# Another order for the seven products of a gate or up matrix, with each PSUM bank's two products eight apart

## Chip, cores and metric

The kernel runs on one core of one Trainium2 chip. The metric is device time in microseconds (us) of one launch, the median of several runs. On the core work five engines with queues of their own: TensorE (PE in the profile, its weight loads PEld), VectorE (DVE), ScalarE (ACT), GpSimd (POOL) and SyncE (SP), which issues most of the transfers.

## What is computed

The reference is a block of two branches on a normalised input of 2048 rows and 576 columns. All inputs are float32.

```python
def _B_ref(x, w_gate, w_up, w_down):
    g = jnp.einsum("bsd,df->bsf", x, w_gate)
    u = jnp.einsum("bsd,df->bsf", x, w_up)
    h = _gelu(g) * u
    return jnp.einsum("bsf,fd->bsd", h, w_down)

xn = _layernorm(x, axis=-1)
s = _A_ref(xn, A_wqkv, A_wo)
g = _silu(_B_ref(xn, B_w_gate, B_w_up, B_w_down))
return x + s * g
```

`_A_ref` is linear attention with 32 heads of 18 columns. `w_gate` and `w_up` are 576 x 4608, `w_down` is 4608 x 576. The change touches only the part with `w_gate` and `w_up`.

## The kernel before

The program has three stages on PE: the attention branch, the gate and up matrices, and the down product. The middle stage is cut into 18 groups of 256 hidden columns. Each group has a gate matrix and an up matrix, so there are 36 matrices in all, numbered `q` from 0 to 35; even `q` is a gate matrix, odd `q` an up matrix.

**One matrix.** A matrix product of 2 x 2 blocks is done with seven block products in place of eight (Strassen's scheme in Winograd's form). `STEPS` (L814) lists the seven as steps `k` = 0 to 6: the name of an accumulator, a weight operand and an input operand. `S1` to `S4` and `T1` to `T4` are sums of blocks. Each step is done for two halves of the rows, `s` = 1 and then `s` = 0, so a matrix is 14 products. In the profile, operands called `xo_` belong to `s` = 1 and those called `xr_` to `s` = 0; weights `wa` hold A11, S1, S2, S3 and weights `wb` hold A12, A22, S4.

**Accumulators.** There are four pairs of PSUM banks: `al`, `be`, `ga`, `de`, one bank of a pair for each `s`. Steps 0 and 4 both add into `al`, steps 2 and 5 into `ga`, steps 3 and 6 into `de`, step 1 alone uses `be`. After the first product of a bank its sum is read and kept, and the second product is then added on top in the bank. `bank_of` (L825) gives each name its banks; `al` and `be` exchange theirs from matrix to matrix.

**PE's order.** `roll` (L832) cuts PE into four groups of 32 rows that work side by side. Each product is 27 matmuls of 32 rows by 512 columns, 6 or 7 for each group of rows. Group 1 begins a product only when group 0 has finished it, and so on, so four or more products are on their way at a time. In one slot every group does one matmul; a product is begun every 6 or 7 slots, and a matrix takes 94 or 95. PE's queue is in order: a matmul that waits holds all four groups.

**Reading a product.** `matrix` (L886) says what follows each product. Let `b` be the bank and `u`, `c22` two SBUF tiles per `s`. Step 0: ACT copies `al` to `u`. Step 1: DVE adds `be` to `u`. Step 2: DVE writes `c22 = u + ga`. Step 3: DVE adds `de` to `c22`, which finishes one block. Step 4 finishes a block from `al`. Steps 5 and 6: DVE adds `u` and `ga`, or `u` and `de`, each of which finishes a block. For a gate matrix "finish" (L919) is an ACT Gelu in place in a tile `h`; for an up matrix (L945) it is a DVE multiply into `h`. In the profile `c22` has the name `h` in a gate matrix and `u` in an up matrix. At step 5 and 6 of an up matrix POOL makes sums of `h` (rows `hs<-h,h`, `h<-h`, `hs<-h,hs`), and SP stores `h` and these sums to `hs_d` in DRAM (rows `hs<-h`, `hs<-hs`) for the down stage.

**Preparing the next matrix.** After certain steps (`run(todo[k])`) the operands of the next matrix are cut into two float32r words: ACT writes the first word, DVE two subtractions of the second (`cut_w`, L786). A11 is cut behind step 0 (`wa<-raw`), S1 to S3 together behind step 3 (`wa<-sm`), A12 and A22 behind step 4 (`wb<-raw`), S4 behind step 5 (`wb<-sm`). POOL forms the sums S (`sm`, L774) and, once per group, sums of `w_down` (`td`, L979).

All operations are pinned to program order on each engine. Tiles and banks are guarded by semaphores: the first matmul into a bank waits until the last reader of that bank is done.

Of the kernel before, what the change touches and what calls it, by code (L numbers as in the profile page):

```python
# [25 lines left out]
TT = TBN // P  # L26
# [39 lines left out]
def block_kernel(ctx, tc, x, xe, xt_d, wq_d, wkv0_d, wkv1_d, wkv2_d, wo, wgu_d, wd_d, out):  # L66
# [8 lines left out]
    def bank_at(i, name):  # L75
        return ps.tile([P, 512], F32, tag=f"bk{i}", bufs=1, name=name)
# [29 lines left out]
    def vec(op, *args, **kw):  # L106
        pin(getattr(nc.vector, op)(*args, **kw))  # L107
# [685 lines left out]
    def mat_pieces(q):  # L793
# [18 lines left out]
        ]  # L812

    STEPS = (  # L814
        ("al", "A11", "B11"), ("be", "S2", "T2"), ("ga", "S1", "T1"), ("de", "S3", "T3"),
        ("al", "A12", "B21"), ("ga", "S4", "B22"), ("de", "A22", "T4"),
    )
    NS = len(STEPS)

    def pairs_of(wn, xn, t, empty):  # L820

        jobs = [(0, 0), (0, 3), (3, 0), (1, 1), (1, 4), (4, 1)]
        return jobs if t == empty else jobs + [(2, 2)]

    def bank_of(q, bk, s):  # L825

        i = SBS.index(s)
        if bk in ("al", "be"):
            return i + (6 if (bk == "al") == (q % 2 == 0) else 0)
        return i + (2 if bk == "ga" else 4)  # L830

    def roll(matrix_of):  # L832

        todo, lens = [], [0] * 4
        for q in range(NQ):
            for k, (bk, wn, xn) in enumerate(STEPS):
                for s in SBS:
                    free = [t for t in range(4) if t not in (W_LO[wn], X_LO[xn])]
                    empty = max(free, key=lambda t: lens[t])
                    jobs = [pairs_of(wn, xn, t, empty) for t in range(4)]  # L840
                    lens = [lens[t] + len(jobs[t]) for t in range(4)]
                    todo.append((q, k, s, jobs))
        rows = [[(p, n) for p, w in enumerate(todo) for n in range(len(w[3][t]))] for t in range(4)]
        begins = [[0] for t in range(4)]
        for q, k, s, jobs in todo:
            for t in range(4):
                begins[t].append(begins[t][-1] + len(jobs[t]))
        skew = [0]
        for t in range(3):
            skew.append(2 + skew[t] + max(  # L850
                begins[t][p + 1] - begins[t + 1][p] for p in range(len(todo))))
        bs, mats = {}, {}
        sems = [tc.alloc_semaphore(f"tile_{t}") for t in range(3)]
        for n in range(skew[3] + len(rows[3])):
            for t in range(4):
                i = n - skew[t]
                if not 0 <= i < len(rows[t]):
                    continue
                p, j = rows[t][i]
                q, k, s, jobs = todo[p]  # L860
                bk, wn, xn = STEPS[k]
                first = t == 0 and j == 0
                if first and k < 4:
                    bs[q, bk, s] = bank_at(bank_of(q, bk, s), f"{bk}_{q}_{s}")
                wi, xi = jobs[t][j]
                last = t == 3 and j == len(jobs[t]) - 1
                r = group(t)
                i = mm(
                    bs[q, bk, s], w_at(q, wn)[r, wi, :], X[s][xn][r, xi, :],
                    start=(first and k < 4), stop=last, skip_group_check=True,  # L870
                    tile_position=(t * KR, 0),
                )
                if t > 0 and j == 0:
                    i._wait_ge(sems[t - 1], p + 1)
                if t < 3 and j == len(jobs[t]) - 1:
                    i.then_inc(sems[t])
                    tc.no_tile_sem_insts.add(i.ins.name)
                    tc.add_to_no_dep_group(f"row_{p}", i.ins)
                if last:
                    tc.declare_fence(i.ins, group=f"row_{p}")  # L880
                if last:
                    if k == 0 and s == SBS[0]:
                        mats[q] = matrix_of(q)
                    mats[q](k, s, bs[q, bk, s])

    def matrix(q, c22, done, todo):  # L886

        u = {}

        def step(k, s, b):  # L890
            if k == 0:
                u[s] = tmp([P, TBN], f"u_{q}_{s}")
                act(u[s], b, AF.Copy)
            elif k == 1:
                vec("tensor_add", u[s], u[s], b)
            elif k == 2:
                vec("tensor_add", c22(s), u[s], b)
            elif k == 3:
                vec("tensor_add", c22(s), c22(s), b)
                done(s, 1, 1, None)  # L900
            elif k == 4:
                done(s, 0, 0, b)
            elif k == 5:
                done(s, 0, 1, (u[s], b))
            else:
                done(s, 1, 0, (u[s], b))
            if s == SBS[-1]:
                run(todo[k])

        return step  # L910
# [206 lines left out]
    def down_all():  # L1117
# [5 lines left out]
        for n in range(N2):  # L1123
            k, g = divmod(n, NG)
            if g == 0 and k in (0, 2, 3, 5):
                accs = [(own_bank if i < 2 else bank)(f"bd_{k}_{i}") for i in range(2 * TT)]
            if g == 0 and k in (1, 4, 5, 6):
                sx[k] = load_sx(k, (14, 15) if k in (1, 5) else (2, 6))
            if k == 6 and g == NG - AHEAD:
                break  # L1130
            load_t(chunk_of(min(n + 8, N2 - 1)) + 1)
            prep_t(chunk_of(min(n + 3, N2 - 1)) + 1)
            prep_s(n + 3)
            down_mm(n, range(2 * TT), accs)
            load_s(n + 6)
            run(late, 2)
            if g < NG - 1:
                continue
            run(late)
            for j in range(2 * TT):  # L1140
                p = accs[j][:, 0:HALF]
                if k == 0:
                    act(u[:, j], p, AF.Copy)
                elif k == 1:
                    yt[k] = yt.get(k) or big(3, [P, 2 * TT, HALF], F32, f"y_{k}")
                    act(yt[k][:, j], p, AF.Silu)
# [299 lines left out]
        return (gate_matrix if q % 2 == 0 else up_matrix)(g, todo)  # L1446

    roll(matrix_of)
    turns["one"] = 0
    load_s(5)  # L1450
    down_all()

# [54 lines left out]
```

## Time and profile before

| what | value |
|---|---|
| median of 3 runs | 1552.02 us (1548.44 to 1553.24) |
| the profiled execution, its own time | 1549.51 us |
| span of the profile in it | 1547.8 us |
| granted TensorE clock | 0.998 |
| gate and up stage, first matmul to the down stage's first | 284.4 to 1139.7 us |
| down stage | 403.6 us |

The profile's rows give start, duration, engine, line, operation, `out<-in` by the program's names without buffer numbers, and in square brackets how long the engine had been idle and what released it. A DVE, ACT or POOL row with "x2" is two instructions in a row. An idle time under 0.15 us is not shown. Since the helpers record each operation, nearly all rows have the helper's line (L104 ACT, L107 DVE, L110 PE, L115 POOL), and one tells them apart by the tiles.

### The profile page before, as it was taken

Reading aid. Unit: us, or ns where it says so; the run is one execution under the profiler, and the core shown is the slowest. Engines: PE = TensorE matmul, PEld = TensorE weight load, DVE = VectorE, ACT = ScalarE, POOL = GpSimd, SP = SyncE. Lnnn points to the kernel's source line nnn. Section 1 sums busy time; section 2 is a strip of 40 time slices with the busy share of each in tenths; the row PEclk is TensorE's granted clock in tenths of the full one; section 3 lists DMA queues with packets and bytes.
Section 4 is the critical chain, followed back from the end, with each engine's and each line's share of the span. In section 5 each row is a group of like instructions: output and inputs, shape, how many; then the busy total and the mean of one; then the engine's idle time right before and its main releaser. Section 6 shows DMA issues by size and latency. Waiting matters only on the chain. (4 is left out here: it accounts for less than half of the span.)

```text
span 1547.8 us, 42471 instructions
## 1 busy us (share of the span) xinstructions
PE 1506.8 (97%) x18431; PEld 1360.0 (88%) x18431; DVE 1044.2 (67%) x1579; ACT 566.5 (37%) x1047; POOL 544.4 (35%) x520
## 2 busy tenths in 40 slices
PE   9999999999999999999999999999999999999998
PEld 8989989888787788778888888877789999999998
DVE  7676566376677776677766776866784565555765
ACT  5444455323222132232233222222234555444443
POOL 5452521243465543555434645435410020000220
PEclk9999999999999999999999999999999999999999
DMA  5354014632344323443423443333578757777773
GB/s 229 127 220 159 1 59 184 252 134 106 128 168 158 143 105 114 156 168 133 151 96 127 169 168 133 114 114 146 202 263 273 241 161 265 244 263 248 276 244 129
DMA packets 114549, 261.97 MB, mean 169 GB/s; under 512 B 10218, under 2 KB 38634, under 8 KB 112314
## 3 DMA queue, kind: packets, MB, share of 16 engines
q1 hardware_dynamic: 112586, 249.95, 45.5%
q0 software_dynamic: 1632, 8.91, 1.6%
q8 instruction: 144, 2.36, 0.6%
q14 instruction: 43, 0.35, 0.1%
q10 hardware_dynamic: 144, 0.39, 0.1%
HBM read 161.27 MB, written 97.91 MB: 167 GB/s over the span
## 5 line engine op out<-in xcount | busy, mean ns | idle before, releaser
L1072 PEld LDWEIGHTS bd<-t,s 128*128 128x128 f32 x3024 | 403.5, 189 | 0.6 <-issue 0.6
L1072 PE MATMUL bd<-t,s 128*128 128x288 f32 x3024 | 403.7, 296 | 0.0
L110 PE MATMUL ga<-xo_B,wb 32*128 32x512 f32 x972 | 258.1, 397 | 17.2 <-DVE h L107 14.6
L110 PE MATMUL de<-xo_T,wa 32*128 32x512 f32 x972 | 259.1, 394 | 10.6 <-DVE u L107 10.6
L110 PE MATMUL al<-xo_B,wb 32*128 32x512 f32 x972 | 265.4, 397 | 0.0
L110 PE MATMUL al<-xr_B,wb 32*128 32x512 f32 x972 | 262.2, 397 | 0.0
L110 PE MATMUL ga<-xr_B,wb 32*128 32x512 f32 x972 | 257.0, 395 | 3.2 <-DVE h L107 3.1
L110 PE MATMUL de<-xr_T,wa 32*128 32x512 f32 x972 | 258.8, 395 | 0.0
L107 DVE TENSOR_TENSOR s<-sr,s 128x512 fp32r<-128x512 f32 x252 | 176.1, 739 | 122.6 <-ACT s L104 118.0
L110 PE MATMUL ga<-xr_T,wa 32*128 32x512 f32 x972 | 253.7, 390 | 0.0
L110 PE MATMUL de<-xr_T,wb 32*128 32x512 f32 x972 | 248.5, 390 | 2.2
L110 PE MATMUL de<-xo_T,wb 32*128 32x512 f32 x972 | 248.7, 390 | 0.0
L110 PE MATMUL ga<-xo_T,wa 32*128 32x512 f32 x972 | 248.3, 387 | 0.0
L110 PE MATMUL al<-xr_B,wa 32*128 32x512 f32 x972 | 248.3, 387 | 0.0
L110 PE MATMUL be<-xr_T,wa 32*128 32x512 f32 x972 | 245.8, 387 | 0.0
L110 PE MATMUL al<-xo_B,wa 32*128 32x512 f32 x972 | 244.4, 386 | 0.0
L110 PE MATMUL be<-xo_T,wa 32*128 32x512 f32 x972 | 243.7, 385 | 0.0
L104 ACT ACTIVATE s<-sr 128x512 fp32r<-128x512 f32 x252 | 149.1, 625 | 193.6 <-PE bd L1072 138.9
L110 PEld LDWEIGHTS ga<-xo_B,wb 32*128 32x128 f32 x972 | 171.4, 183 | 39.5 <-DVE h L107 22.2
L110 PEld LDWEIGHTS de<-xr_T,wb 32*128 32x128 f32 x972 | 175.3, 183 | 23.2 <-DVE h L107 9.9
L110 PEld LDWEIGHTS de<-xo_T,wa 32*128 32x128 f32 x972 | 174.0, 183 | 22.7 <-DVE u L107 17.8
L110 PEld LDWEIGHTS ga<-xr_B,wb 32*128 32x128 f32 x972 | 172.7, 183 | 23.5 <-DVE h L107 10.9
(174 smaller groups left out, 4245.9 us busy)
## 6 DMA issues: line engine op xcount, KB each, us to landing
sr<-hs SPq DMA_DIRECT2D x252, 256.0 KB
hs<-h SPq DMA_DIRECT2D x68, 512.0 KB
raw<-in_wgu_dram SPq DMA_DIRECT2D x36, 768.0 KB
hs<-hs SPq DMA_DIRECT2D x102, 256.0 KB
td<-in_wd_dram SPq DMA_DIRECT2D x18, 576.0 KB
td<-td SPq DMA_DIRECT2D x18, 576.0 KB
tr<-td SPq DMA_DIRECT2D x16, 576.0 KB
tr<-in_wd_dram SPq DMA_DIRECT2D x12, 576.0 KB
```

The source lines that it names most:

```text
L104: pin(nc.scalar.activation(*args, **kw))
L107: pin(getattr(nc.vector, op)(*args, **kw))
L110: i = nc.tensor.matmul(*args, **kw)
L1072: nc.tensor.matmul(banks[j][:, 0:HALF], hw[n, s][:, a, t * P : (t + 1) * P], w[:, c, g % 4], start=(new and g == 0 and m == 0), stop=(g == ...
```

## The change

`STEPS` gets another order: the product S2 x T2 with its accumulator `be` moves from step 1 to step 3, and the `ga` and `de` products of steps 2 and 3 move up to steps 1 and 2. Now `al` has steps 0 and 4, `ga` 1 and 5, `de` 2 and 6, `be` 3. Between the two products of a bank there were 8 (`al`) or 6 (`ga`, `de`) products of PE's order from start to start, and now there are 8 for each. `bank_of` gives the pairs of banks in turn, moved on by one pair from matrix to matrix; from the last use of a pair to its use in the next matrix there are then 8 products as well.

The readers follow: `c22` begins as an ACT copy of `ga`, DVE adds `de` to it at step 2, and at step 3 DVE adds `be` to `u` and then `u` to `c22`. The down stage names its banks 0 to 7 in order, as the last matrix frees them.

```diff
     STEPS = (
-        ("al", "A11", "B11"), ("be", "S2", "T2"), ("ga", "S1", "T1"), ("de", "S3", "T3"),
+        ("al", "A11", "B11"), ("ga", "S1", "T1"), ("de", "S3", "T3"), ("be", "S2", "T2"),
         ("al", "A12", "B21"), ("ga", "S4", "B22"), ("de", "A22", "T4"),
     )
...
-    def bank_of(q, bk, s):
-
-        i = SBS.index(s)
-        if bk in ("al", "be"):
-            return i + (6 if (bk == "al") == (q % 2 == 0) else 0)
-        return i + (2 if bk == "ga" else 4)
+    def bank_of(q, k, s):
+
+        return 2 * ((k - q) % 4) + SBS.index(s)
...
             elif k == 1:
+                act(c22(s), b, AF.Copy)
+            elif k == 2:
+                vec("tensor_add", c22(s), c22(s), b)
+            elif k == 3:
                 vec("tensor_add", u[s], u[s], b)
-            elif k == 2:
-                vec("tensor_add", c22(s), u[s], b)
-            elif k == 3:
-                vec("tensor_add", c22(s), c22(s), b)
+                vec("tensor_add", c22(s), c22(s), u[s])
                 done(s, 1, 1, None)
...
-                accs = [(own_bank if i < 2 else bank)(f"bd_{k}_{i}") for i in range(2 * TT)]
+                accs = [bank_at(i, f"bd_{k}_{i}") for i in range(2 * TT)]
```

What moves in the queues is shown at two places. The first is DVE in the up matrix 15, from the cut of A11 for the next matrix up to the cut of S1 to S3. Names carry group, half and buffer number: `u_15_1` is the tile `u` of matrix 15 for `s` = 1, `u22_7_1` is its `c22` (of group 7), and `be_15_1` is the bank. Before:

```order
L107 TENSOR_TENSOR u_15_1_9865<-u_15_1_9865,be_15_1_9743 128x512
L107 TENSOR_TENSOR u_15_0_9896<-u_15_0_9896,be_15_0_9777 128x512
L107 TENSOR_TENSOR u22_7_1_9980<-u_15_1_9865,ga_15_1_9808 128x512
L107 TENSOR_TENSOR u22_7_0_10006<-u_15_0_9896,ga_15_0_9839 128x512
L107 TENSOR_TENSOR u22_7_1_9980<-u22_7_1_9980,de_15_1_9875 128x512
L107 TENSOR_TENSOR h_7_1_1_9423<-h_7_1_1_9423,u22_7_1_9980 128x512
L107 TENSOR_TENSOR u22_7_0_10006<-u22_7_0_10006,de_15_0_9905 128x512
L107 TENSOR_TENSOR h_7_0_1_9425<-h_7_0_1_9425,u22_7_0_10006 128x512
L107 TENSOR_TENSOR wa_2921<-sm_16_9860,wa_2921 128x3x256
```

The same place on DVE after the change:

```order
L107 TENSOR_TENSOR u22_7_1_9958<-u22_7_1_9958,de_15_1_9840 128x512
L107 TENSOR_TENSOR u22_7_0_9984<-u22_7_0_9984,de_15_0_9871 128x512
L107 TENSOR_TENSOR u_15_1_9893<-u_15_1_9893,be_15_1_9903 128x512
L107 TENSOR_TENSOR u22_7_1_9958<-u22_7_1_9958,u_15_1_9893 128x512
L107 TENSOR_TENSOR h_7_1_1_9453<-h_7_1_1_9453,u22_7_1_9958 128x512
L107 TENSOR_TENSOR u_15_0_9924<-u_15_0_9924,be_15_0_9937 128x512
L107 TENSOR_TENSOR u22_7_0_9984<-u22_7_0_9984,u_15_0_9924 128x512
L107 TENSOR_TENSOR h_7_0_1_9455<-h_7_0_1_9455,u22_7_0_9984 128x512
L107 TENSOR_TENSOR wa_2921<-sm_16_9888,wa_2921 128x3x256
```

The number of DVE operations is the same. Behind the last of the first four products there were four operations up to the cut, and now there are six, in two chains of three that depend on each other; two of the adds have both inputs in SBUF.

The second place is ACT in the gate matrix 16, from the copy of `al` to the first word of S1 to S3 for the next matrix. Before:

```order
L104 ACTIVATE u_16_1_10322<-al_16_1_10108 128x512
L104 ACTIVATE u_16_0_10353<-al_16_0_10143 128x512
L104 ACTIVATE wa_2921<-raw_17_10129 128x384
L104 ACTIVATE h_8_1_1_10319<-h_8_1_1_10319 128x512
L104 ACTIVATE h_8_0_1_10321<-h_8_0_1_10321 128x512
L104 ACTIVATE wa_2921<-sm_17_10313 128x3x384
```

The same place on ACT after the change:

```order
L104 ACTIVATE u_16_1_10356<-al_16_1_10142 128x512
L104 ACTIVATE u_16_0_10387<-al_16_0_10177 128x512
L104 ACTIVATE wa_2921<-raw_17_10163 128x384
L104 ACTIVATE h_8_1_1_10353<-ga_16_1_10213 128x512
L104 ACTIVATE h_8_0_1_10355<-ga_16_0_10256 128x512
L104 ACTIVATE h_8_1_1_10353<-h_8_1_1_10353 128x512
L104 ACTIVATE h_8_0_1_10355<-h_8_0_1_10355 128x512
L104 ACTIVATE wa_2921<-sm_17_10347 128x3x384
```

Two copies from the banks `ga` have come in ahead of the Gelu of the same tiles; they write the tiles `h` one step earlier than DVE did.

More of the change, by code (lines that the diff above doesn't have):

```diff
@@ L814, in block_kernel @@
     STEPS = (
-        ("al", "A11", "B11"), ("be", "S2", "T2"), ("ga", "S1", "T1"), ("de", "S3", "T3"),
+        ("al", "A11", "B11"), ("ga", "S1", "T1"), ("de", "S3", "T3"), ("be", "S2", "T2"),
         ("al", "A12", "B21"), ("ga", "S4", "B22"), ("de", "A22", "T4"),
     )
-    NS = len(STEPS)
     def pairs_of(wn, xn, t, empty):
@@ L863, in roll @@
                 if first and k < 4:
-                    bs[q, bk, s] = bank_at(bank_of(q, bk, s), f"{bk}_{q}_{s}")
+                    bs[q, bk, s] = bank_at(bank_of(q, k, s), f"{bk}_{q}_{s}")
                 wi, xi = jobs[t][j]
@@ L1448, in block_kernel @@
     roll(matrix_of)
-    turns["one"] = 0
     load_s(5)
```

## The prediction

> **What bounds the kernel now.** I read the page first, then the groups of PE by line, the timeline of PE for one gate and one up matrix, and the timelines of DVE and POOL beside them. The first fence has the page's head and its engine line, then two rows of PE's groups (busy, mean ns, idle before and who ended it), then where the stage with the change begins (the first `al` matmul at 284.4) and ends (the chain of waits: the first `bd` matmul).
>
> ```profile
> span 1547.8 us, 42471 instructions
> PE 1506.8 (97%) x18431; PEld 1360.0 (88%) x18431; DVE 1044.2 (67%) x1579; ACT 566.5 (37%) x1047; POOL 544.4 (35%) x520
> L110 PE MATMUL ga<-xo_B,wb 32*128 32x512 f32 x972 | 258.1, 397 | 17.2 <-DVE h L107 14.6 <-DVE u L107 0.2
> L110 PE MATMUL de<-xo_T,wa 32*128 32x512 f32 x972 | 259.1, 394 | 10.6 <-DVE u L107 10.6
> L110 PE MATMUL al<-xo_B,wa x972: 382/385/497, 284.4 to 1118.1; 32*128 32x512 f32 x195
> 1139.74 403.63 PE bd L1072 x3024
> ```
>
> PE is busy 97% of the span, but its matmuls overlap, so this share hides lost time. The stage takes 1139.74 - 284.4 = 855.3 us for 36 matrices. PE's own idle time there is put down to DVE: 17.2 us before the second `ga` product, 10.6 before the first `de` product. The timeline of PE shows the true loss, from the first matmul of gate matrix 16 on.
>
> ```profile
> 660.07 0.39 PE L110 MATMUL al<-xo_B,wa 32*128 32x512 f32 x1
> 670.19 0.49 PE L110 MATMUL de<-xo_T,wa 32*128 32x512 f32 x1 [0.62 <-DVE u L107]
> 677.51 0.49 PE L110 MATMUL ga<-xo_B,wb 32*128 32x512 f32 x1 [0.89 <-DVE h L107]
> 677.85 0.39 PE L110 MATMUL ga<-xo_B,wb 32*128 32x512 f32 x1
> 684.90 0.39 PE L110 MATMUL al<-xo_B,wa 32*128 32x512 f32 x1
> 691.02 0.39 PE L110 MATMUL ga<-xo_T,wa 32*128 32x512 f32 x1
> 694.19 0.39 PE L110 MATMUL de<-xo_T,wa 32*128 32x512 f32 x1
> 700.62 0.49 PE L110 MATMUL ga<-xo_B,wb 32*128 32x512 f32 x1
> 707.25 0.39 PE L110 MATMUL al<-xo_B,wa 32*128 32x512 f32 x1
> ```
>
> In the up matrix from 684.90 to the first `de` matmul at 694.19 nothing waits: 41 slots in 9.29 us, 0.2266 us a slot. A gate matrix has 95 slots, an up matrix 94, so without waits they would take 21.53 and 21.30 us. They take 24.83 and 22.35: 3.30 and 1.05 us are lost, **4.35 us a pair, 78 us for 18 pairs**. In the gate matrix the first 41 slots take 10.12, so the wait at 670.19 costs 0.83, and 0.11 more for restarting (677.51 to 677.85 is 0.34 where a slot is 0.23). The other 2.36 lie behind 677.51, at steps 5 and 6. All that the up matrix loses lies at steps 5 and 6 too (700.62 to 707.25 is 26 slots, 5.89, in 6.63 us, and 0.31 is lost ahead of 700.62).
>
> The next fence has DVE in order of time, from step 3 of up matrix 15 into gate matrix 16, and then from step 3 of that gate matrix to the first reads of the next up matrix.
>
> ```profile
> 656.28 0.69 DVE L107 TENSOR_TENSOR u<-u,de 128x512 f32<-128x512 f32 x1 [1.10 <-PE de L110]
> 657.00 0.69 DVE L107 TENSOR_TENSOR h<-h,u 128x512 f32<-128x512 f32 x1
> ...
> 658.56 0.69 DVE L107 TENSOR_TENSOR h<-h,u 128x512 f32<-128x512 f32 x1
> 659.17 1.52 DVE L107 TENSOR_TENSOR wa<-sm,wa 128x768 fp32r<-128x768 f32 x2
> 660.72 1.28 DVE L107 TENSOR_TENSOR h<-h,al 128x512 f32<-128x512 f32 x2
> 662.20 1.13 DVE L107 TENSOR_TENSOR wb<-raw,wb 128x512 fp32r<-128x512 f32 x2 [0.20 <-ACT wb L104]
> 663.36 0.69 DVE L107 TENSOR_TENSOR u<-u,ga 128x512 f32<-128x512 f32 x1
> ...
> 665.40 1.29 DVE L107 TENSOR_TENSOR h<-h,u 128x512 f32<-128x512 f32 x1
> 666.61 2.80 DVE L107 TENSOR_TENSOR wb<-sm,wb 128x256 fp32r<-128x256 f32 x2
> 669.45 0.69 DVE L107 TENSOR_TENSOR u<-u,de 128x512 f32<-128x512 f32 x1
> ...
> 682.43 0.69 DVE L107 TENSOR_TENSOR h<-h,de 128x512 f32<-128x512 f32 x1 [1.10 <-PE de L110]
> 684.92 2.62 DVE L107 TENSOR_TENSOR wa<-sm,wa 128x768 fp32r<-128x768 f32 x2 [1.80 <-ACT wa L104]
> 687.56 1.47 DVE L107 TENSOR_TENSOR wb<-raw,wb 128x256 fp32r<-128x256 f32 x4
> 689.06 1.28 DVE L107 TENSOR_TENSOR h<-u,ga 128x512 f32<-128x512 f32 x2
> 691.46 0.73 DVE L107 TENSOR_TENSOR wb<-sm,wb 128x256 fp32r<-128x256 f32 x2 [1.11 <-ACT wb L104]
> ...
> 699.88 0.69 DVE L107 TENSOR_TENSOR u<-u,ga 128x512 f32<-128x512 f32 x1 [0.40 <-PE ga L110]
> ```
>
> Two kinds of wait are to be seen. At 699.88 DVE had been idle: it read `ga` as soon as the product begun at 691.02 was done, ended at 700.57, and PE went on at 700.62. Six products (41 slots) after 691.02 is 700.31, so a distance of six leaves 0.43 us for a read of 0.69. This wait is built in. At 669.45 it is another thing: DVE has worked without a break since 662.20, and the read of `de` that PE waits for at 670.19 ends at 670.14. That is a **backlog of DVE**, in spite of a distance of eight.
>
> **The change part by part.** *Steps 5 and 6.* With 54 slots from use to use, PE comes back to the bank of 691.02 at 703.26, 3.38 us after the product is done at 699.88, and a read of 0.69 fits. What is lost at steps 5 and 6 goes: 2.36 + 1.05 = **3.41 us a pair**. Late next is whichever DVE read stands behind a backlog; there are two.
>
> *The wait at step 3 of the gate matrix* remains, now for `be`. It is still the up matrix's step 6 that it waits for. In the up matrix two adds moved from steps 1 and 2, where DVE is idle at times, to step 3. A dependent operation follows after 0.72 (656.28 to 657.00), an independent one after 0.61 (658.56 to 659.17). Six operations in two chains take 0.72 + 0.72 + 0.61 + 0.72 + 0.72 + 0.61 = 4.10 us from the first's start to the cut, where the trace has 659.17 - 656.28 = 2.89: 1.21 later. The idle 0.20 at 662.20 takes a part back, so 1.01 reaches 669.45. PE also comes earlier by what it no longer loses at the up matrix's step 6, about half of the 0.74 above. The wait becomes 0.83 + 1.01 + 0.37 = 2.21, with the restart 2.32, where it was 0.94: **+1.38 a pair**.
>
> *Step 2 of the up matrix* gets a wait of its own. PE waits there for the first `h<-u,ga` at 689.06, the gate matrix's step 5. From DVE's first work on the gate matrix's last step-3 product (682.43) to its end (689.75) it is 7.32 us, and PE came at 691.02, 1.22 after it, with 0.05 from DVE to PE. PE will come 0.38 earlier, since the step-6 wait behind 682.43 goes (it is about a sixth of the 2.36), and later by one slot in the new order: 1.07 is left. The chain gets one more dependent add, 0.72. Then 0.35 is spare, if nothing else grows. The ends: POOL can draw out both `c22` adds and the cuts behind them, as the next fence shows.
>
> ```profile
> 664.85 1.29 POOL L115 TENSOR_TENSOR hs<-h,h 128x512 f32<-128x512 f32 x1 [14.97 <-DVE h L107]
> 666.22 1.62 POOL L115 TENSOR_TENSOR h<-h 128x512 f32<-128x512 f32 x1
> 667.91 2.63 POOL L115 TENSOR_TENSOR hs<-h,h 128x512 f32<-128x512 f32 x2
> ...
> 679.68 1.00 POOL L115 TENSOR_TENSOR sm<-raw,sm 128x384 f32<-128x384 f32 x1
> 683.07 4.06 POOL L115 TENSOR_TENSOR td<-td 128x288 f32<-128x288 f32 x4 [2.39 <-DMA td<-in_wd_dram]
> ```
>
> Beside POOL's work the DVE multiply at 665.40 takes 1.29 where that at 657.00 takes 0.69, and the two cuts at 666.61 take 2.80 where those at 691.46 take 0.73; `u<-u,de` at 669.45, which reads a bank, keeps its 0.69. So an add from SBUF can grow by 0.60 and a pair of cuts by 2.07. POOL's chain hangs on the multiply ahead of 664.85 and shifts by the same 1.01, so `sm` would end at 681.7 and `td` at 688.1. The first `c22` add falls on the end of `sm`, and the first `wb<-raw` cut on the end of `td`. The wait lies between 0 and 0.60 + 2.07 - 0.35 = 2.3. I take 0.9 (one add and about a third of the cuts' growth), with its restart 1.01: **+1.00 a pair**.
>
> The Trainium skill, "SBUF — State Buffer", section "Who interferes with whom", says that a DVE instruction with two inputs in SBUF is blocked by a GpSimd instruction that reads SBUF, and one with at most one such input is not. The trace agrees by the rows just named, and by this rule the change has a price of its own, since two adds lose their PSUM input. If the rule held both adds for a whole `sm` row of 1.00 each, the wait would be 2.0 - 0.35 = 1.65 in place of 0.9, and the total some 13 us less gain.
>
> *ACT's copies.* 72 more. They are off the path: ACT is busy 37%, and the copy of `al` takes 0.60.
>
> ```profile
> 669.20 0.60 ACT L104 ACTIVATE u<-al 128x512 f32<-128x512 f32 x1 [4.15 <-PE al L110]
> 672.28 0.79 SPq L118 DMA_DIRECT2D hs<-h x2
> 677.74 0.61 SPq L118 DMA_DIRECT2D td<-in_wd_dram  x1
> ```
>
> But the copy writes `h` one step earlier than DVE did, so it must find the store of the group before (`hs<-h`) landed. It is counted at nothing as long as that is so (fourth rival).
>
> *The down stage* gets its banks in the order in which they come free, as before: nothing. Into it DVE carries the two adds of the last up matrix once:
>
> ```profile
> 1130.00:1145.00 15.00, 15.00 (x122) 12.81 (x115) 14.42 (x23) 4.20 (x7) 3.60 (x7) 0.79 0.70 241
> ```
>
> DVE is busy 14.42 of these 15 us (third figure), so 1.2 us are lost. The first gate matrix has no backlog ahead of it and saves about as much.
>
> **Sum.** -3.41 + 1.38 + 1.00 = -1.03 us a pair, 18 pairs: -18.5 us. The profiled execution took 1549.51 (1.7 around its span); that gives 1531. The median shown is 1552.02, 2.5 above, so on its footing I predict **1533.5**.
>
> **The rivals.** *The forecast* (the two waits remain, the second between 0.3 and 1.6): 1521 to 1545. Chance 0.57. For it: both chains can be counted in rows, and the six-product waits have no other cause.
>
> *The second wait doesn't come.* If POOL's sums fall beside DVE's reads of PSUM, 0.35 stays spare: -3.41 + 1.38 = -2.03, -36.5 us, 1515.5. Chance 0.17. Against it: `td` already overlaps the `wa` cuts at 684.92 (2.62 against 1.52 at 659.17).
>
> *Slower.* `td` comes to lie on the four cuts at 687.56, which ran undisturbed in 1.47. It starts when its load lands, and the load stands in SP's queue behind the stores that shift by 1.01. With a wait of 2.3 and a draw-out of the adds the pair is at +0.4, 1559. It decides from a wait of 1.9 on, where the pair comes out even. Chance 0.11.
>
> *The copies wait for the stores, so the waits at step 5 aren't removed.* The second `hs<-h` is issued by 673.07. The longest landing that I can bound is that of the load behind it, 677.74 to POOL's start on it at 683.07, 5.33 us. With the shift of 1.01 the copy could end at 680.0; PE is due at that bank, 75 slots and the 2.3 of step 3 after 660.07, at 679.4. A loss of 0.6 a pair leaves -7 us, and 1.0 a pair, where the landing is 0.4 longer, leaves no change: 1541 to 1552. Chance 0.15.
>
> **How the numbers follow.** A change of 0.3% (4.7 us, about what a measurement can tell) separates the three. Faster holds the forecast, the second rival and a third of the fourth: 0.78. Same holds most of the rest of the fourth and the edge of the third: 0.12. Slower 0.10. The range leaves out the tail of the third rival and a few us at the low end: 1517 to 1553.
>
> **What would show it.** In the new profile a gate matrix should take 23.9 us (95 slots and 2.3) and an up matrix 22.3. PE should have no idle time before the second `ga` and `de` products; idle time of about 2.1 us before `be<-xo_T,wa`, ended by DVE `u`, in 17 gate matrices; and some 0.8 before `de<-xo_T,wa`, ended by DVE `h`, in up matrices. ACT `h<-ga` should be released by PE, not by a DMA. The prediction is wrong in its mechanism if PE still waits at step 5, and in its sizes if the cuts at the head of the up matrix are drawn out far beyond 2.62 and 1.47.

## The result, and the profile after

The changed kernel takes **1534.88 us** (median of 4 runs, 1532.59 to 1536.59); the kernel before, on the same chip, 1550.23 (4 runs). The ratio is 0.9898, 95% interval 0.9873 to 0.9923: 1.0% faster, 15.3 us. The forecast was 1533.5. The profiled execution took 1536.59 us, the slowest of the four, so the profile's difference (spans 1534.5 against 1547.8, 13.3 us) is a little smaller than that of the medians.

First the page of the changed kernel: the head, and the two groups of PE's matmuls in the stage that still have idle time before them.

```profile
span 1534.5 us, 42454 instructions
...
L110 PE MATMUL be<-xo_T,wa 32*128 32x512 f32 x972 | 248.0, 389 | 28.6 <-DVE u L107 28.6
L110 PE MATMUL de<-xo_T,wa 32*128 32x512 f32 x972 | 255.9, 393 | 10.0 <-DVE h L107 9.9
```

The 17.2 us before the second `ga` product are gone. In their place `be` of step 3 waits 28.6 us for DVE's `u` (the gate matrices) and `de` of step 2 waits 10.0 us for DVE's `h` (the up matrices). Those are the two places, and the releasers, that were named. PE's timeline shows the lengths: from the first matmul of gate matrix 16 through up matrix 17 to the head of matrix 18.

```profile
651.12 0.38 PE L110 MATMUL al<-xo_B,wa 32*128 32x512 f32 x1
662.36 0.49 PE L110 MATMUL be<-xo_T,wa 32*128 32x512 f32 x1 [1.69 <-DVE u L107]
674.93 0.38 PE L110 MATMUL al<-xo_B,wa 32*128 32x512 f32 x1
682.39 0.49 PE L110 MATMUL de<-xo_T,wa 32*128 32x512 f32 x1 [1.15 <-DVE h L107]
697.92 0.38 PE L110 MATMUL al<-xo_B,wa 32*128 32x512 f32 x1
```

The gate matrix takes 23.81 us, the up matrix 22.99. The up matrices differ (21.31 to 22.99); over up matrices 1 to 33 the mean is 22.38. The same subtraction of first `al` matmuls gives this table for every kernel of the study (means; gate matrices 2 to 34, up matrices 1 to 33; without waits 21.53 and 21.30):

| kernel | gate, us | up, us | median, us |
|---|---|---|---|
| before | 24.81 | 22.38 | 1548.7 to 1551.0 by chip |
| changed | 23.80 | 22.38 | 1534.9 |
| e1 order alone | 29.41 | 25.39 | 1689.7 |
| e2 S4 cut late | 22.31 | 22.36 | 1510.3 |
| e3 td sums late | 23.80 | 21.31 | 1515.2 |
| e4 before, S4 cut late | 25.42 | 22.36 | 1561.9 |
| e5 c22 apart | 23.80 | 22.36 | 1533.9 |
| e6 S4 cut late, c22 apart | 21.59 | 21.90 | 1490.1 |
| e7 S4 cut late, td late, c22 apart | 21.60 | 21.31 | **1480.5** |
| e8 before, S4 and A11 cuts late | 24.07 | 22.35 | 1536.9 |
| e9 before, all of these edits | 24.11 | 22.35 | 1537.7 |
| e10 t cut late | 23.81 | 22.38 | 1538.6 |
| e11 e7, t cut late | 21.61 | 21.31 | 1482.7 |

The next fence is DVE's timeline of the changed kernel: the end of up matrix 15, gate matrix 16 as far as the read that step 3 waits for, and the head of up matrix 17.

```profile
647.52 0.69 DVE L107 TENSOR_TENSOR u<-u,be 128x512 f32<-128x512 f32 x1 [0.62 <-PE be L110]
...
651.63 1.51 DVE L107 TENSOR_TENSOR wa<-sm,wa 128x768 fp32r<-128x768 f32 x2
...
658.79 2.79 DVE L107 TENSOR_TENSOR wb<-sm,wb 128x256 fp32r<-128x256 f32 x2
661.62 0.69 DVE L107 TENSOR_TENSOR u<-u,de 128x512 f32<-128x512 f32 x1
...
672.04 1.37 DVE L107 TENSOR_TENSOR h<-h,u 128x512 f32<-128x512 f32 x1
...
676.48 2.04 DVE L107 TENSOR_TENSOR wa<-sm,wa 128x768 fp32r<-128x768 f32 x2 [1.75 <-ACT wa L104]
678.54 3.08 DVE L107 TENSOR_TENSOR wb<-raw,wb 128x256 fp32r<-128x256 f32 x4
681.65 1.28 DVE L107 TENSOR_TENSOR h<-u,ga 128x512 f32<-128x512 f32 x2
```

From the first step-3 add to the cut it is 651.63 - 647.52 = 4.11 us. The read `u<-u,de` ends at 662.31 and PE goes on at 662.36. At the up matrix's head the four `wb<-raw` cuts take 3.08 us, where before they took 1.47. The reason is in the timelines of POOL, SP and ACT at the same place:

```profile
677.14 3.89 POOL L115 TENSOR_TENSOR td<-td 128x288 f32<-128x288 f32 x4 [4.28 <-DMA td<-in_wd_dram]
...
670.33 0.70 SPq L118 DMA_DIRECT2D td<-in_wd_dram  x1
...
668.47 0.60 ACT L104 ACTIVATE h<-ga 128x512 f32<-128x512 f32 x1 [2.42 <-DMA hs<-h]
```

The `td` sums begin 2.2 us after the up matrix (before, 1.8 us ahead of it), and so lie on the cuts. And ACT's copy of `ga` was held by a store, against the sign that I had given.

Last, the head of the down stage in PE's timeline, and the granted clock in two stretches behind its second wait (the third number from the end, PEclk):

```profile
1120.90 4.05 PE L1068 MATMUL bd<-t,s 128*128 128x288 f32 x18
1127.36 0.92 PE L1068 MATMUL bd<-t,s 128*128 128x288 f32 x5 [2.41 <-DVE u L107]
1129.41 1.81 PE L1068 MATMUL bd<-t,s 128*128 128x288 f32 x6 [1.13 <-DVE u L107]
...
1129.40:1133.00 3.60, 3.59 (x15) 3.59 (x16) 3.57 (x5) 1.15 (x2) 2.13 (x4) 0.50 1.01 375
1133.00:1137.50 4.50, 4.50 (x28) 4.50 (x28) 4.50 (x9) 1.80 (x3) 0.00 (x0) 0.73 1.03 396
```

The stage runs from 284.5 to 1120.9, 836.4 us against 855.3: 18.9 us less. The down stage loses 3.5 us in these two waits. Half the clock is not peculiar to it, and not a consequence of these waits alone: the kernel before has no wait there and runs its head at 0.50 too,

```profile
1140.00:1144.00 4.00, 4.00 (x18) 4.00 (x18) 3.86 (x7) 0.00 (x0) 1.49 (x3) 0.50 0.82 299
```

for 6.83 us in all (1138.77 to 1145.60). The changed kernel has 10.2 us of it, 3.41 from 1121.75 on, which is before the first wait, and 6.82 from 1128.58 on. At half the clock the 3.4 us more cost some 1.7. From the down stage's first matmul to its last the rows by line give, for the changed kernel and then for the one before:

```profile
L1068 PE MATMUL bd<-t,s x3024: 288/294/609, 1120.9 to 1529.8; 128*128 128x288 f32 x189
```

```profile
L1072 PE MATMUL bd<-t,s x3024: 287/295/607, 1139.7 to 1543.1; 128*128 128x288 f32 x189
```

408.9 against 403.4 us: 5.5 us given back, of which the waits and the clock make 5.2. -18.9 + 5.5 = -13.4 is the difference of the spans, to 0.1.

### The profile page after: what moved, and what is told of

It is laid out like the page before. It is cut to its first block, busy times and chain, and to the rows that moved or that the text cites. A ratio compares the mean times of both kernels' runs of the same rounds, so it can differ in the third digit from the quotient of the medians.

```text
span 1534.5 us, 42454 instructions
## 1 busy us (share of the span) xinstructions
PE 1484.4 (97%) x18431; PEld 1392.7 (91%) x18431; DVE 1063.6 (69%) x1579; ACT 604.9 (39%) x1119; POOL 548.1 (36%) x520
## 4 chain that ended last, share of the span: by engine, by line
PE 70%; DVE 25%; issue 2%; ACT 1%; DMA 1%; SPq 0%; ACTq 0%
PE bd L1068 26%; PE be L110 9%; DVE h L107 8%; PE kv L110 7%; PE de L110 7%; PE al L110 7%; DVE wb L107 7%; DVE u L107 6%; PE ga L110 5%; PE s L110 3%; PE q L110 3%; DVE wa L107 3%; PE kv_a L110 1%; ACT wa L104 1%; DMA x<-in_xe_dram 0%
## 5 line engine op out<-in xcount | busy, mean ns | idle before, releaser
L110 PE MATMUL be<-xo_T,wa 32*128 32x512 f32 x972 | 248.0, 389 | 28.6 <-DVE u L107 28.6
L110 PE MATMUL al<-xr_B,wa 32*128 32x512 f32 x972 | 256.6, 391 | 0.0
L110 PE MATMUL de<-xr_T,wa 32*128 32x512 f32 x972 | 246.9, 387 | 0.0
L110 PE MATMUL ga<-xr_B,wb 32*128 32x512 f32 x972 | 244.0, 385 | 0.0
L110 PE MATMUL de<-xo_T,wb 32*128 32x512 f32 x972 | 243.4, 384 | 0.0
L110 PE MATMUL al<-xo_B,wb 32*128 32x512 f32 x972 | 243.4, 384 | 0.0
L110 PE MATMUL al<-xr_B,wb 32*128 32x512 f32 x972 | 243.1, 384 | 0.0
L110 PE MATMUL ga<-xo_B,wb 32*128 32x512 f32 x972 | 243.0, 384 | 0.0
L110 PEld LDWEIGHTS be<-xo_T,wa 32*128 32x128 f32 x972 | 175.1, 183 | 46.9 <-DVE u L107 35.8
L110 PEld LDWEIGHTS de<-xo_T,wa 32*128 32x128 f32 x972 | 172.6, 183 | 22.1 <-DVE h L107 17.2
L110 PEld LDWEIGHTS be<-xr_T,wa 32*128 32x128 f32 x972 | 176.4, 183 | 10.9 <-DVE u L107 5.5
L110 PEld LDWEIGHTS de<-xr_T,wa 32*128 32x128 f32 x972 | 176.4, 183 | 5.6
```

What stands on the lines that cost most here:

```text
L110: i = nc.tensor.matmul(*args, **kw)
```

## The experiments

My theory: distance decides what DVE's delay costs. Six products leave no time for a read, eight leave some 3 us; what is left in the changed kernel are backlogs, in each case made by a nameable piece of work ahead of the read. The rivals: the order and ACT's copies bring the gain whatever the banks; or the remaining waits come from the added chain itself.

**e1: the new order with the old banks.**

```diff
-    def bank_of(q, k, s):
-        return 2 * ((k - q) % 4) + SBS.index(s)
+    def bank_of(q, bk, s):
+        i = SBS.index(s)
+        if bk in ("al", "be"):
+            return i + (6 if (bk == "al") == (q % 2 == 0) else 0)
+        return i + (2 if bk == "ga" else 4)
...
```

> The new order with the banks as they were before (al and be change places from matrix to matrix, ga and de keep theirs). Theory (distance decides): the four reuses that were six products apart at steps 5 and 6 are eight apart now, but ga and de of the next matrix come six products after their last use, at steps 1 and 2, where DVE is fuller. In a gate matrix the read of the last ga product ends 5.1 us after the matrix's start, and PE is due there at 2.95; the last de product is read by 11.2 and PE would be due at 8.4. PE then stands about 3.2 us (14 slots) further back than in the changed kernel when step 2 begins. In an up matrix the read of the gate's ga product ends at 7.4 us, PE is due at 2.9: again about 3.2 us more. Some 6.4 us a pair, 115 us in all: about 1650 us, surely above 1600, with PE idle before the first ga and de products. Rival 1 (the order and ACT's copies bring the gain, the banks do not matter): 1535 us. Rival 2 (a distance of six costs what it cost before, wherever it stands): 3.4 us a pair, 1590 us or less.

Measured: 1689.69 us, ratio 1.0904 (1.0883 to 1.0925), 9% slower than before. PE's groups by line, then DVE's timeline at the head of a gate matrix that begins at 719.09, then the clock in a part of it:

```profile
L110 PE MATMUL ga<-xo_T,wa 32*128 32x512 f32 x972 | 298.8, 436 | 70.2 <-DVE u L107 35.7 <-DVE h L107 34.5
L110 PE MATMUL de<-xo_T,wa 32*128 32x512 f32 x972 | 261.4, 405 | 47.3 <-DVE u L107 36.8 <-DVE h L107 10.5
```

```profile
723.48 0.69 DVE L107 TENSOR_TENSOR u<-u,ga 128x512 f32<-128x512 f32 x1
...
726.43 0.69 DVE L107 TENSOR_TENSOR u<-u,ga 128x512 f32<-128x512 f32 x1 [1.53 <-PE ga L110]
```

```profile
724.20:732.00 7.80, 5.61 (x60) 4.23 (x64) 6.15 (x7) 0.53 (x1) 6.79 (x5) 0.76 0.65 226
```

The waits stand where they were expected, before the first `ga` and `de` products, and both rivals fall: the order alone is no gain at all. It is worse than the 1650 expected. The rows show two things that were not counted; how much each adds was not worked out. DVE, full as it is, stands idle for 1.53 us until 726.43, for the last matmuls of the product that it has to read next: PE had waited 2.10 us, until 724.32, and while it waited, these matmuls stood still behind it. And the granted clock is 0.76 behind the wait.

**e2: the changed kernel, with the cut of S4 behind step 6.**

```diff
-            [lambda: cut_w(wt["b"][:, 3:4], sm[:, 3:4], "S4")],
             [],
+            [lambda: cut_w(wt["b"][:, 3:4], sm[:, 3:4], "S4")],
...
```

> The changed kernel with the cut of S4 for the next matrix run behind step 6 of each matrix, not step 5, so that DVE reads the last de products first. Theory (what is left at step 3 of the gate matrix is a backlog: the read of de stands behind a cut of 2.8 us): the read comes about 2.8 us earlier, the wait of 1.85 us with its restart goes, and a gate matrix takes 21.6 to 22.0 us in place of 23.8. If the up matrix's wait stays as it is, 17 x 2.0 = 34 us less: 1500 us, between 1492 and 1510. Rival 1 (the wait is that of the two moved adds and of POOL's hold on them, not of the cut's place): no more than 0.3 us a gate, 1530 us or more. Rival 2 (the up matrix's wait takes the gain, since POOL's sums do not move): its wait grows by as much as PE comes earlier, 1530 us.

Measured: 1510.31 us, ratio 0.9742 (0.9727 to 0.9758). `be` waits no more, and 24.6 us are gained on the changed kernel's median: the read stood behind the cut. But 34 were expected. ACT's groups by line, one of the copies in gate matrix 22, and PE behind it:

```profile
L104 ACT ACTIVATE h<-ga 128x512 f32<-128x512 f32 x36 | 21.6, 599 | 80.3 <-DMA hs<-h 48.8 <-PE de L110 18.1 <-PE ga L110 9.5
...
791.36 0.60 ACT L104 ACTIVATE h<-ga 128x512 f32<-128x512 f32 x1 [4.69 <-DMA hs<-h]
```

```profile
792.01 0.50 PE L110 MATMUL ga<-xr_B,wb 32*128 32x512 f32 x1 [0.82 <-ACT h L104]
```

With the wait at step 3 gone, a new one is bare: the copy writes `h`, which SP is still storing for the group before, and PE waits for the copy at step 5.

**e3: the changed kernel, with POOL's `td` sums behind the sums for the next gate matrix.**

```diff
-            todo[3].append(lambda: down_sums(g))
+            if g == NG - 1:
+                todo[3].append(lambda: down_sums(g))
+        elif g < NG - 1:
+            todo[0].append(lambda: down_sums(g))
```

> The changed kernel with POOL's sums of the down weights (td) put behind the sums of the up matrix's successor, so that they no longer run beside the cuts at the head of the up matrix; the last group keeps its place. Theory (the wait at step 2 of the up matrix is the draw-out of the four wb cuts by POOL, 3.1 in place of 1.5 us, and of the wa cuts, 2.0 in place of 1.5): the cuts take 1.5 and 1.5 us again, the wait of 0.75 with its restart and most of the 1.06 us that an up matrix loses go; 17 x 0.9 = 15 us less: 1519 us, 1514 to 1526. Rival (the wait comes from the longer chain of c22 adds alone, POOL only fills time): 1532 to 1537 us, with the same idle time before de.

Measured: 1515.22 us, ratio 0.9785 (0.9764 to 0.9807). PE's group, then DVE's timeline at the end of gate matrix 16 and the head of up matrix 17, which begins at 666.61:

```profile
L110 PE MATMUL de<-xo_T,wa 32*128 32x512 f32 x972 | 250.3, 389 | 0.6 <-DVE h L107 0.6
```

```profile
663.74 1.34 DVE L107 TENSOR_TENSOR h<-h,u 128x512 f32<-128x512 f32 x1
...
668.17 1.54 DVE L107 TENSOR_TENSOR wa<-sm,wa 128x768 fp32r<-128x768 f32 x2 [1.75 <-ACT wa L104]
669.72 1.47 DVE L107 TENSOR_TENSOR wb<-raw,wb 128x256 fp32r<-128x256 f32 x4
671.22 1.28 DVE L107 TENSOR_TENSOR h<-u,ga 128x512 f32<-128x512 f32 x2
```

Every up matrix takes 21.31 us, no time is lost in them, and the gate matrices stay at 23.80. So the wait at step 2 of the up matrix was the draw-out of the cuts by `td`: with `td` elsewhere, the longer chain of the new order costs nothing there. The gain is 4.7 us larger than the 15 expected; the down stage, 404.0 us here against 408.9, makes up about that much (see e10). The `c22` add at 663.74 is drawn out here too (1.34), and the `wa` cut begins 1.56 us after the matrix, as in the changed kernel (676.48 - 674.93 = 1.55): the hold on the add costs nothing.

**e4: the kernel before, with the cut of S4 behind step 6** (the diff of e2).

> The kernel before with the cut of S4 run behind step 6, not step 5. Theory (two kinds of wait: the one at step 3 of the gate matrix is a backlog of DVE, those at steps 5 and 6 are built in by the distance of six products): only the first goes, 0.94 us in 17 gate matrices, 16 us: 1534 us, a gate matrix takes 23.9 us, an up matrix 22.35 as it was, and PE stays idle before the second ga product. Rival 1 (all these waits are backlog, so the place of the cut moves them all): 4 us a pair, 1480 us. Rival 2 (the wait at step 3 is built in too): 1550 us.

Measured: 1561.94 us, ratio 1.0073 (1.0057 to 1.009): slower. The expectation failed. PE's groups, DVE in gate matrix 16 (it begins at 663.94), and PE at the wait of step 5, there and one gate matrix later:

```profile
L110 PE MATMUL ga<-xo_B,wb 32*128 32x512 f32 x972 | 267.7, 409 | 34.9 <-DVE h L107 32.8
```

```profile
673.88 2.81 DVE L107 TENSOR_TENSOR wb<-sm,wb 128x256 fp32r<-128x256 f32 x2
676.72 2.77 DVE L107 TENSOR_TENSOR wa<-raw,wa 128x256 fp32r<-128x256 f32 x2
...
680.72 0.68 DVE L107 TENSOR_TENSOR h<-u,ga 128x512 f32<-128x512 f32 x1
```

```profile
681.46 0.49 PE L110 MATMUL ga<-xo_B,wb 32*128 32x512 f32 x1 [1.92 <-DVE h L107]
...
682.06 0.62 PE L110 MATMUL al<-xo_B,wb 32*128 32x512 f32 x1
...
685.43 0.40 PE L110 MATMUL ga<-xo_B,wb 32*128 32x512 f32 x1
...
729.81 0.50 PE L110 MATMUL ga<-xo_B,wb 32*128 32x512 f32 x1 [1.90 <-DVE h L107]
```

The wait at step 3 went, as the theory has it. But the late cut now runs right ahead of that of A11, both drawn out beside POOL's sums, and the read of `ga` behind them is the one that six products leave no time for: the idle time before the second `ga` product doubles, 17.2 to 34.9 us. That alone only moves the loss. The rest is the clock: in 8 of these 17 gate matrices a stretch of some 3.4 us at half speed follows the wait (682.06 to 685.43), and they take 26.0 us in place of 24.9. I had not counted what stands ahead of the next read.

**e5: the changed kernel, with `c22` of a gate matrix in a tile of its own.**

```diff
...
         def done(s, f, b, src):
             o = hid[s, b][:, f]
             if src is None:
-                src = o
+                src = c22[s]
...
-        return matrix(2 * g, lambda s: hid[s, 1][:, 1], done, todo)
+        return matrix(2 * g, take, done, todo)
```

> The changed kernel with c22 of a gate matrix kept in a temporary tile, as the up matrix does it, and not in h, which the Gelu then writes from it. ACT's copy of ga no longer overwrites a tile that the group before is still storing. Theory (the copy waits for the store in part of the gate matrices, but ends 1.3 us before PE needs the bank, behind the wait at step 3): nothing changes on the path, 1535 us, within 3 us; ACT's copies in gate matrices are released by PE. Rival (the held copy keeps ACT's queue back, and the cuts and Gelus behind it): 5 to 10 us less.

Measured: 1533.89 us, ratio 0.9896 (0.9877 to 0.9915): no change. ACT's copies (now `g<-ga`) are released by PE:

```profile
L104 ACT ACTIVATE g<-ga 128x512 f32<-128x512 f32 x36 | 21.6, 600 | 27.7 <-PE ga L110 27.1 <-ACT wa L104 0.6
```

In the changed kernel the copies' wait for the store lies wholly beneath the wait at step 3.

**e6: e2 and e5 together.**

```diff
-            [lambda: cut_w(wt["b"][:, 3:4], sm[:, 3:4], "S4")],
             [],
+            [lambda: cut_w(wt["b"][:, 3:4], sm[:, 3:4], "S4")],
...
-        return matrix(2 * g, lambda s: hid[s, 1][:, 1], done, todo)
+        return matrix(2 * g, take, done, todo)
```

> The cut of S4 behind step 6 and c22 of a gate matrix in a temporary tile. Theory (with the wait at step 3 gone the cover of the store is gone too: PE then waited at step 5 of the gate matrix for ACT's copy, which waited for the store, 10.5 us over 11 gate matrices): these 10.5 us go, and PE, coming up to 0.9 us earlier in them, gives up to 5 of them back in the up matrix: 1503 us, 1498 to 1508, no idle time of PE before the ga product of step 5. Rival (the copy is late because ACT is, not because of the store): 1510 us as with the late cut alone.

Measured: 1490.13 us, ratio 0.9612 (0.9586 to 0.9637). Gate matrices take 21.59 us, so the store was the cause of e2's shortfall. The gain is 13 us larger than expected, since the up matrices improve too, to 21.90, where a loss was expected. `td` starts when its load lands, 24.8 to 25.8 us after the gate matrix's start in two pairs looked at, 26.0 (677.14 - 651.12) in the changed kernel. With a gate matrix 2.2 us shorter it starts later in the up matrix, and only part of the cuts is left for it to draw out. In 12 of the 17 up matrices 22.1 us remain. In the one that begins at 741.25 the `wa` cuts take 1.54 us, undisturbed, but `td` starts at 744.46, on the `wb` cuts (744.16, 3.10 us). In the one that begins at 784.93 it starts at 789.15, when the `wb` cuts (787.89, 1.47 us) are all but over, and the matrix takes 21.31.

**e7: e2, e3 and e5 together.**

```diff
+            [lambda: cut_w(wt["b"][:, 3:4], sm[:, 3:4], "S4")],
...
+            todo[0].append(lambda: down_sums(g))
...
+        return matrix(2 * g, take, done, todo)
```

> The cut of S4 behind step 6, td's sums behind the sums of the up matrix's successor, and c22 of a gate matrix in a temporary tile. Theory (the three causes are separate, and with distances of eight nothing else is short): a gate matrix at 21.6 us, an up matrix at 21.3, against 23.80 and 22.36 in the changed kernel, 3.2 us a pair, 17.5 pairs, 56 us less: 1479 us, 1474 to 1486. Rival (POOL's chain in the gate matrix, which does not move, sets the head of the up matrix once PE is earlier): a wait at step 2 of the up matrix remains, 1490 us or more.

Measured: 1480.52 us, ratio 0.9555 (0.9535 to 0.9575), 4.5% faster than before and the best version found. PE's groups:

```profile
L110 PE MATMUL be<-xo_T,wa 32*128 32x512 f32 x972 | 243.0, 384 | 0.0
L110 PE MATMUL de<-xo_T,wa 32*128 32x512 f32 x972 | 243.0, 384 | 0.0
```

No wait of PE is left in the stage; gate and up matrices are at 21.60 and 21.31, within 0.1 us of their slots.

**e8: the kernel before, with the cut of S4 behind step 6 and that of A11 behind step 2.**

```diff
-            [lambda: cut_w(wt["a"][:, 0:1], rv[:, 0, 0:1], "A11")],
-            [], [],
+            [], [],
+            [lambda: cut_w(wt["a"][:, 0:1], rv[:, 0, 0:1], "A11")],
...
-            [lambda: cut_w(wt["b"][:, 3:4], sm[:, 3:4], "S4")],
             [],
+            [lambda: cut_w(wt["b"][:, 3:4], sm[:, 3:4], "S4")],
...
```

> The kernel before with the cut of S4 behind step 6 and the cut of A11 behind step 2, not step 0. With the late cut of S4 alone the kernel before became 12 us slower: the wait at step 3 of the gate matrix went, and that at step 5 grew from 0.98 to 1.98 us. Theory (the cut of A11 then runs right behind that of S4, both drawn out to 2.8 us beside POOL, and DVE's read of the first ga product stands behind both): with A11's cut behind that read the growth goes and the step-3 wait stays away, a gate matrix takes 23.9 us: 1534 us, 1530 to 1540. Rival (the read of ga is late for another reason, such as the store of h that it overwrites): 1555 us or more.

Measured: 1536.92 us, ratio 0.9918 (0.9898 to 0.9937). That settles e4: with A11's cut away from the read of `ga` the old order gains the step-3 wait, 13 us, and keeps waits at steps 5 and 6.

**e9: the kernel before, with the edits of e8, e3 and e5.**

```diff
+            [lambda: cut_w(wt["a"][:, 0:1], rv[:, 0, 0:1], "A11")],
...
+            [lambda: cut_w(wt["b"][:, 3:4], sm[:, 3:4], "S4")],
...
+            todo[0].append(lambda: down_sums(g))
...
+        return matrix(2 * g, take, done, todo)
```

> The kernel before with all the edits that take the other waits away: the cut of S4 behind step 6, that of A11 behind step 2, td's sums behind the sums of the up matrix's successor, c22 of a gate matrix in a temporary tile. The same surroundings bring the changed order to 1480.5 us with no wait of PE left in the stage. Theory (a distance of six products loses 3.4 us a pair whatever else is cleared): 18 x 3.4 = 61 us above that, 1541 us, 1530 to 1546, with gate matrices of about 24.1 and up matrices of 22.35 us. Rival (the waits at steps 5 and 6 are backlog of DVE and POOL too, so clearing the queues removes them): 1510 us or less.

Measured: 1537.65 us, ratio 0.9914 (0.9894 to 0.9935). PE's group with most idle time:

```profile
L110 PE MATMUL de<-xo_T,wb 32*128 32x512 f32 x972 | 248.5, 390 | 16.0 <-DVE g L107 16.0
```

The old order loses 2.5 us in a gate and 1.04 in an up matrix (24.11 and 22.35, against 21.60 and 21.31 in e7): 3.55 a pair. Between these two kernels lie 1537.7 - 1480.5 = 57 us; in its own surroundings the change brought 15. But the old order's queue is not clear yet in the gate matrix. DVE there, in gate matrix 16:

```profile
675.80 2.21 DVE L107 TENSOR_TENSOR wa<-raw,wa 128x256 fp32r<-128x256 f32 x2
678.04 0.69 DVE L107 TENSOR_TENSOR g<-g,de 128x512 f32<-128x512 f32 x1
```

The first `de` product of this matrix is done at 676.9. Its read stands behind A11's cut, which the edit of e8 put there, and comes 1.1 us late. So some 1.1 of the 2.5 us is backlog, and the 57 us are not the price of the distance alone: with no backlog that price is nearer 1.4 in a gate matrix and 1.04 in an up matrix. An old order without this cut in the way was not run.

**e10 and e11: the first cut of the down weights behind step 6 of the last up matrix**, in the changed kernel and in e7. DVE had stood idle before this cut in both.

```diff
-            todo[2].append(lambda: prep_t(1))
...
-            todo[6].append(lambda: prep_s(3))
+            todo[6] += [lambda: prep_t(1), lambda: prep_s(3)]
```

> The changed kernel with the first cut of the down weights (t) run behind step 6 of the last up matrix, not step 2; nothing else is moved. In the changed kernel DVE stood idle for 1.35 us before that cut, which waited for its load, with the six step-3 operations of the last up matrix queued behind it, and the down stage lasted 5.5 us longer than before (3.5 us of idle time of PE, the rest at a lower granted clock behind it). Theory (the new order put the step-3 reads behind this cut): the idle time of PE before bd goes from 3.5 to under 1.0 us, and the down stage from its first bd matmul to its last from 408.9 to 404 to 406 us; the whole 1531 us, 1528 to 1534. Rival (DVE's work in the last up matrix, two adds more, makes the idle time by itself): 408 us or more for the down stage and 1535 us.

> The kernel with the late cut of S4, the late td sums and c22 apart (1480.5 us), and the first cut of the down weights behind step 6 of the last up matrix. Theory: there DVE stood idle for 1.99 us before that cut; the idle time of PE before bd goes from 3.3 us to under 1.0, the whole is 1477 us, 1474 to 1479. Rival (that idle time has another cause): 1480 us.

Measured: 1538.61 us, ratio 0.9937 (0.9919 to 0.9954), and 1482.73, ratio 0.9574 (0.956 to 0.9588): no gain, if anything a loss of 2 to 4 us (the intervals overlap those without the edit). The theory fails. PE's group of e10, and DVE's read that PE had waited for at the head of the down stage (which begins at 1121.37):

```profile
L1068 PE MATMUL bd<-t,s 128*128 128x288 f32 x3024 | 404.9, 296 | 6.4 <-DVE u L107 4.3 <-DVE t L107 2.1
```

```profile
1125.11 0.68 DVE L107 TENSOR_TENSOR u<-u,de 128x512 f32<-128x512 f32 x1
```

The read does come earlier: it ends 4.4 us after the stage's start, where PE had gone on with it at 6.5 (1127.36 - 1120.90). But PE now waits for the `t` cut as well, and for `u` no less: with the cut late it has only 6 matmuls to do ahead of its first wait, where it had 18 in the changed kernel.

Two other runs say more of the 5.5 us. In e3 and e5 the `t` cut and the chain of step 3 stand as in the changed kernel, but DVE was not idle before the cut, since its load came in time. Their down stages take 404.0 and 407.0 us (1103.3 to 1507.3 and 1120.3 to 1527.3), with 0.7 and 3.0 us of idle time. So the longer chain by itself need cost no more than 0.6 us over the 403.4 of before. That the late load makes the rest is likely, but e5 lies between, and what sets it there stays open.

## Why the prediction was right, point by point

*Steps 5 and 6 (-3.41 a pair).* Right in effect, and shown: these waits are gone in the changed kernel, and e1 shows that the banks are as needed as the order. But that they "have no other cause" than the distance holds for the up matrix only. In gate matrix 16 of the kernel before, DVE has

```profile
672.73 2.82 DVE L107 TENSOR_TENSOR wa<-raw,wa 128x256 fp32r<-128x256 f32 x2
...
676.78 0.68 DVE L107 TENSOR_TENSOR h<-u,ga 128x512 f32<-128x512 f32 x1
```

and the first `ga` product is done at 675.94: DVE, with no break since A11's cut, reads it 0.84 us late. The first gate matrix, which has no such backlog, loses 22.98 - 21.53 = 1.45 us. So the distance alone costs some 1.45 + 1.05 = 2.5 us a pair, and about 0.9 of the 3.41 was backlog. The forecast didn't suffer, because the 3 us of slack take up both.

*The wait at step 3 of the gate matrix (+1.38).* Right. From the first add to the cut 4.11 us were measured for 4.10, and a gate matrix loses 23.80 - 21.53 = 2.27 us for 2.32. e2 shows that the read stands behind the cut of S4.

*Step 2 of the up matrix (+1.00).* The size is right, the up matrices after the first take 22.44 us on the mean and so lose 1.14; the parts are not. I had the first `c22` add drawn out by `sm` (0.60) and a third of the cuts' growth. The add is drawn out (1.37) at no cost, and the whole of `td` lies on the cuts: 0.52 on the `wa` and 1.61 on the `wb` cuts, against a spare time of some 0.8 us in e3 (the first of the two reads of `ga` ends at about 671.9, PE takes the bank 27 slots, 6.12 us, after 666.61). So the collision of the third rival did take place; the load left SP 1.5 us later in the gate matrix than before and was 1.5 us longer on its way. It did not decide, since the wait stayed at 1.15 in this pair, below the 1.9 named there.

"Who interferes with whom" in "SBUF — State Buffer" of the Trainium skill is borne out as to the hold: the two-input add (1.37) and cuts (3.08 for 1.47) grow beside POOL, the reads of banks keep 0.69. The price of 13 us that the prediction worked out for it did not appear, since the held add was not on the path.

*ACT's copies (nothing).* Right in price (e5), wrong in its sign: they are held by stores in many gate matrices. The fourth rival's mechanism was there, under the cover of the step-3 wait, and appeared as soon as e2 took the cover away.

*The down stage (nothing on balance).* Wrong in size. I had 1.2 us of lost time, paid for by the first gate matrix. Measured were 5.5: 3.5 us of idle time, and 3.4 us more at half the clock than before. Against it stand the first gate and the first up matrix, which save 1.5 us (22.98 to 21.44) and 1.07 (22.37 to 21.31): no backlog stands ahead of the one, and in the other the cuts that `td` draws out are the `wa` cuts alone (2.59 us; the `wb` cuts keep 1.47).

*The number.* That 1533.5 came so near to 1534.88 is partly luck. The forecast was a change of -18.5 us, against -15.3 by the medians and -13.3 by the profiles. It was put on a median of 1552.02 from 3 runs; the kernel before came to 1550.23 in 4.

## What to carry to other kernels

Count for each buffer how many steps lie between its uses, and compare the time left between "done" and "due" with the read: where nothing is left, every delay in the reader's queue is paid in full, and tidying that queue leaves what the read itself lacks; where some is left, it takes up small delays, and tidying can remove the rest. A change that gives such slack shows its worth only when the next wait in line is taken away too (15 us alone, 57 us between e9 and e7), so list what is late next, and look below each wait for others that it hides. Before moving work behind a critical read, look at what it then stands ahead of.

## What the runs showed of the hardware that was not expected

A short wait of PE can cost more than its length: in e4 a wait of 1.92 us was followed by matmuls of 0.62 us in place of 0.39 from 682.06 to 685.43, while after one of 1.90 us a pair later the clock stayed full:

```profile
680.00:686.00 6.00, 4.54 (x52) 3.65 (x56) 2.40 (x5) 0.00 (x0) 4.50 (x5) 0.72 0.97 361
...
728.40:734.40 6.00, 4.40 (x68) 3.17 (x72) 2.73 (x5) 0.63 (x1) 4.48 (x5) 1.00 1.00 362
```

The waits of 1.69 us in the changed kernel's gate matrices left it at 1.00. The traces show what decides. The times at which the granted clock changes lie on a grid of 3.413 us: in e4, the drops at 681.96 and 777.53 are 28 steps apart, those at 777.53 and 873.11 again 28. Cut the stage from its second matrix on into the windows of this grid. In e4, 8 windows with 1.89 to 2.09 us of PE idle time are followed by a drop, in e1 27 with 1.90 to 2.11. No other window at full clock is; the most idle of those has 1.89 us, the next 1.85. The wait of 1.92 us lies within one window (678.55 to 681.96). That of 1.90 us (727.91 to 729.81) runs over the edge at 729.75, so that one window has 1.84 us of it, and the clock stays. The bound of some 1.9 us is read off these two kernels alone, and it does not cover the heads of stages: ahead of the down stage of the changed kernel the clock falls with PE never idle, though with few matmuls (33 in the 5 us from 1116, where the 6 us from 1110 have 100).

The Trainium skill, "TensorE: Matmul & The Clock Gate", section "The HAM clock gate", puts the drop after an idle window of about 3.4 us, and lets the windows run freely. The grid of 3.413 us and the length of the slow stretch, 3.37 us, agree; that a whole window must be idle does not.
